# Splitting two small matmul passes in a DMA-fed start-up, and giving the last Q blocks four PSUM banks

## The chip, the cores and the metric

The kernel runs on one core of a Trainium2 chip. The metric is the device time of that core in microseconds (us). Most runs of one kernel agree within 0.3%.

## The reference, cut to what matters

One transformer block on 2048 tokens of width 1024, in bf16: linear attention with 32 heads, then a gated MLP, both with a layernorm whose scale and shift come from a condition vector.

```python
mod = (silu(c) @ w_mod)                         # six rows of 1024: sa, ca, ga, sb, cb, gb
h = layernorm(x) * (1 + ca) + sa
q, k, v = split(h @ wqkv)
pq, pk = phi(q), phi(k)                         # phi(t) = where(t > 0, t + 1, exp(t)) + 1e-6
kv = einsum('bhsd,bhse->bhde', pk, v); z = pk.sum(s)
o = (pq @ kv) / (pq @ z + 1e-6)
x = x + ga * (o @ wo)
h = layernorm(x) * (1 + cb) + sb
x = x + gb * ((gelu(h @ w_gate) * (h @ w_up)) @ w_down)
```

## The kernel before

Every instruction is put in its engine's stream in program order; a wait is added wherever an instruction touches bytes that another engine or a transfer wrote or still reads. So the order of the lines below is the order on TensorE.

**Start-up.** Nothing can be multiplied before weights and x have come from memory. The scale and shift of the first layernorm are needed as columns (one value per partition), in four quarters of 256 features. Quarter `q` has two weight tiles, 512 KB each: shift (`t` = 0, issued first) and scale (`t` = 1). A column pass is 32 matmuls with one column each (shortened here, as all code of this document):

```python
def mod_cols(q, bank, ts=(1, 0)):               # scale first, then shift
    for t in ts:
        for b in range(2):
            col = MC0 + q * 4 + t * 2 + b
            for dc in range(NDC):               # 8
                matmul(PS(bank, col, col + 1), WMQ[q][:, dc, t, b*P:(b+1)*P], SILUT[:, dc:dc+1], ...)
```

`mod_copy(q)` (VectorE) takes the four columns out of PSUM, and `mod1` (VectorE) scales and shifts the transposed h1T. Only then may the K matmuls of this quarter's two 128-feature slices (`dc` = 2q, 2q+1) run. The transfers are issued in this order: ..., wmq2 (shift, scale), wk 4, wk 5, wmq3 (shift, scale), wk 6, wk 7, wv (first half of its columns in two pieces, then the second half, 1 MB), x of chunks 4 to 7, wq. The end of the start-up, where `k_tiles` and `k_part` are K matmuls of some slices and `kb0` says which bank each K tile of chunks 0 to 3 is collected in:

```python
k_part(0, [3]); k31([2, 3])
mod_cols(2, 4)
mod_copy(2, 4)
k_tiles([3], [(2, 0), (2, 1)])
k_tiles([2, 3], [(3, 0)])
mod1(0, 1, 4, 5); mod1(1, 3, 4, 5); mod1(0, 4, 5, 6)
k_tiles([4, 5], [(0, 0), (0, 1), (1, 0), (1, 1)])
k_tiles([4], [(2, 0), (2, 1)])
mod_cols(3, 4)
mod_copy(3, 4)
mod1(0, 1, 6, 8); mod1(1, 3, 6, 8)
k_tiles([5], [(2, 0), (2, 1)])
k_tiles([4, 5], [(3, 0)])
for (c_, jg), b in kb0.items(): kv_mm(c_, "k", jg, b, [6, 7])     # 14 matmuls
k31([4, 5, 6, 7]); k31(list(range(NDC)), MC0, 512)                # k31: chunk 3, second half of K
# ... evictions of K ...
for c_ in range(4):                              # V tiles: (chunk, half of the columns)
    for vc, jg in (((0, 0), (1, 0)), ((0, 1), (1, 1)), ((2, 0), (2, 1)), ((3, 0), (3, 1)))[c_]:
        b = nb(); kv_mm(vc, "v", jg, b, range(NDC)); v_evac(vc, jg, b)
    # ... kvacc(c_ - 1) if c_ >= 1
```

**The last Q blocks.** PSUM has eight banks; banks 5 to 7 hold the accumulated KV until VectorE has copied it out (kvbd). It is then transposed by a DMA (kvt), and W2 = KV x wo is made, two banks a pair. `den` is the denominator pq @ z for two of the four groups of 512 tokens (a "pair" of groups); VectorE takes its reciprocal, which comes back broadcast by DMA (`rb_load`) for `pq_scale`. `wo_chunk` multiplies 128 tokens of pq with W2. Twelve Q blocks are still to do, ten of them after `kvt`; a Q block is 8 matmuls into one bank, followed by ScalarE's exponential and two VectorE instructions (the last of them is `pq`):

```python
def q_next(evac=True):
    sg, qc = q_todo.pop(0)
    b = (0, 1, 2, 3)[qn[0]] if qn[0] < 4 else qn[0] % 2     # from the fifth on: banks 0 and 1
    qn[0] += 1
    q_block(sg, qc, evac, b)

first_q = q_next(False); kvacc(NCH - 1); zcols(); q_evac(*first_q)
q_next()
den(0, 3); kvbd(); kvt(); rb_load(0); rb_load(1)
q_next(); q_next()
for u in range(NG):                              # 8
    q_next()
    if u >= 2: w2_pair(u - 2 + (u == 7))         # banks 2 and 3
    if u == 6: w2_pair(5, 4)                     # banks 4 and 5
    # ... pq_scale on VectorE
w2_pair(NG - 1, 4)
# ...
for c_ in range(12):
    wo_chunk(c_, 6 if c_ == 0 else 2 * (c_ % 2)) # two banks a chunk
    if c_ == 0: den(1, 4); rb_load(2)
```

Of the kernel before, what the change touches and what calls it, by code (L numbers as in the profile page):

```python
# [18 lines left out]
NG = 8  # L19
# [195 lines left out]
def bass_adaLN_cond__linear_attn_block__geglu_ffn__prompt_kernel(  # L215
# [15 lines left out]
    with ExitStack() as es:  # L231
# [85 lines left out]
        def r_sm(name):  # L317
            return [(SMO[name], SMO[name] + SMSZ[name], name)]
# [13 lines left out]
        def r_h1(sg, k0=0, k1=NDC, s0=0, s1=SGW):  # L332
            return r_t8(H1O[sg], f"h1T{sg}", k0, k1, s0, s1)
# [7 lines left out]
        def r_w(off, name, dc, c0=0, c1=D):  # L341
            return [(off + (dc * D + c0) * 2, off + (dc * D + c1) * 2, name)]
# [14 lines left out]
        def r_wmq(i, t):  # L357
            return [(MSO[i] + (dc * 2 + t) * 512, MSO[i] + (dc * 2 + t + 1) * 512, f"wmq{i}") for dc in range(NDC)]
# [33 lines left out]
        def pr(b):  # L392
            return [(b * 2048, (b + 1) * 2048)]

        def PS(b, c0=0, c1=512):
            return ps_all[:, b * 512 + c0: b * 512 + c1]
# [187 lines left out]
        def mod1(c0, n, dc0=0, dc1=NDC):  # L584
            sg, ci = divmod(c0, CPG)
            mods(H1, r_h1, sg, sc1, ci * P, (ci + n) * P, dc0, dc1, "h1")
# [8 lines left out]
        def mod_cols(q, bank, ts=(1, 0)):  # L595
            o = None
            rng = [(bank * 2048 + (MC0 + q * 4) * 4, bank * 2048 + (MC0 + q * 4 + 4) * 4)]
# [3 lines that stand above are left out]
                    for dc in range(NDC):  # L601
                        o = sch.op(T, lambda e, t=t, b=b, dc=dc, col=col: e.matmul(
                            PS(bank, col, col + 1), WMQ[q][:, dc, t, b * P:(b + 1) * P], SILUT[:, dc:dc + 1],
                            start=(q == b == dc == 0 and t == 1), stop=(dc == NDC - 1), skip_group_check=True),
                            rd=r_wmq(q, t) + r_sm("siluT"), pwr=(rng if dc == 0 else ()), note=f"mod{q}.{t}.{b}.{dc}")
            for t_ in rng:
                sch.ps.set_writer(t_[0], t_[1], o)

        def mod_copy(q, bank):
            rng = [(bank * 2048 + (MC0 + q * 4) * 4, bank * 2048 + (MC0 + q * 4 + 4) * 4)]  # L610
            sch.op(V, lambda e: e.tensor_tensor(MODT[:, q * 4:q * 4 + 4], PS(bank, MC0 + q * 4, MC0 + q * 4 + 4), ADD4[:, :], ALU.add),
                   prd=rng, rd=r_sm("add4"), wr=r_smc("modt", q, 16), note=f"modcp{q}")
# [65 lines left out]
        def kv_mm(c_, kind, jg, bank, dcs):  # L678
            sg, ci = divmod(c_, CPG)
            W_, off, name = (WK, OFF_WK, "wk") if kind == "k" else (WV, OFF_WV, "wv")  # L680
            o = None
            for dc in dcs:
                o = sch.op(T, lambda e, dc=dc: e.matmul(PS(bank), H1[sg][:, dc, ci * P:(ci + 1) * P], W_[:, dc, jg * 512:(jg + 1) * 512],  # L683
                                                        start=(dc == 0), stop=(dc == NDC - 1)),
                           rd=r_h1(sg, dc, dc + 1, ci * P, (ci + 1) * P) + r_w(off, name, dc, jg * 512, (jg + 1) * 512),
                           pwr=(pr(bank) if dc == 0 else ()), note=f"{kind} c{c_} jg{jg} dc{dc}")
            if dcs[-1] == NDC - 1:
                pset_writer(bank, o)
# [26 lines left out]
        def nb():  # L715
            b = bank_i[0] % bank_i[1]
            bank_i[0] += 1
            return b
# [37 lines left out]
        def k31(dcs, c0=0, c1=MC0):  # L756
            rng = [(4 * 2048 + c0 * 4, 4 * 2048 + c1 * 4)]
            for dc in dcs:
                o = sch.op(T, lambda e, dc=dc: e.matmul(PS(4, c0, c1), H1[0][:, dc, 3 * P:4 * P], WK[:, dc, 512 + c0:512 + c1],
                                                        start=(c0 > 0 and dc == 0), stop=(dc == NDC - 1), skip_group_check=True),  # L760
                           rd=r_h1(0, dc, dc + 1, 3 * P, 4 * P) + r_w(OFF_WK, "wk", dc, 512 + c0, 512 + c1),
                           pwr=(rng if dc == 0 else ()), note=f"k c3 jg1 dc{dc} {c0}")
            if dcs[-1] == NDC - 1:
                sch.ps.set_writer(*rng[0], o)

        def k_tiles(dcs, tiles):
            for dc in dcs:
                for c_, jg in tiles:
                    kv_mm(c_, "k", jg, kb0[c_, jg], [dc])
# [47 lines left out]
        mod1(3, 1, 0, 4)  # L817
        k_part(0, [3])
        k31([2, 3])
        mod_cols(2, 4)  # L820
        mod_copy(2, 4)
        k_tiles([3], [(2, 0), (2, 1)])
        k_tiles([2, 3], [(3, 0)])
        mod1(0, 1, 4, 5)
        mod1(1, 3, 4, 5)
        mod1(0, 4, 5, 6)
        k_tiles([4, 5], [(0, 0), (0, 1), (1, 0), (1, 1)])
        k_tiles([4], [(2, 0), (2, 1)])
        mod_cols(3, 4)
        mod_copy(3, 4)  # L830
        mod1(0, 1, 6, 8)
        mod1(1, 3, 6, 8)
        k_tiles([5], [(2, 0), (2, 1)])
        k_tiles([4, 5], [(3, 0)])
        for (c_, jg), b in kb0.items():
            kv_mm(c_, "k", jg, b, [6, 7])
        k31([4, 5, 6, 7])
        k31(list(range(NDC)), MC0, 512)
        for (c_, jg), b in kb0.items():
            k_evac(c_, jg, b)  # L840
# [1 line left out]
        for c_ in range(4):  # L842
            for vc, jg in (((0, 0), (1, 0)), ((0, 1), (1, 1)), ((2, 0), (2, 1)), ((3, 0), (3, 1)))[c_]:
                b = nb()
# [58 lines left out]
        for c_ in range(4, NCH):  # L903
# [23 lines left out]
            for jg in range(2):  # L927
                b = nb()
# [3 lines left out]
            for jg in range(2):  # L932
                b = nb()
# [37 lines left out]
        def w2_pair(g, b0=2):  # L971
            for half in range(2):
                b = b0 + half
                sch.op(T, lambda e, b=b, half=half: e.matmul(PS(b), KVT[:, g, :], WO[:, g, half * 512:(half + 1) * 512], start=True, stop=True),  # L974
                       rd=R_KVT + [(OFF_WS + g * 2048 + half * 1024, OFF_WS + g * 2048 + (half + 1) * 1024, "wo")], pwr=pr(b), note=f"w2 {g}.{half}")
            sch.op(A, lambda e: e.activation(W2[:, g, :], ps_all[:, b0 * 512:(b0 + 2) * 512], ACTF.Copy),
                   prd=pr(b0) + pr(b0 + 1), wr=r_w(OFF_WK, "w2", g), note=f"w2cp{g}")
# [44 lines left out]
        qn = [0]  # L1022

        def q_next(evac=True):
            sg, qc = q_todo.pop(0)
            b = (0, 1, 2, 3)[qn[0]] if qn[0] < 4 else qn[0] % 2
            qn[0] += 1
            q_block(sg, qc, evac, b)
            return sg, qc, b
# [13 lines left out]
        for u in range(NG):  # L1043
            q_next()
            if u >= 2:
                w2_pair(u - 2 + (u == 7))
            if u == 6:
                w2_pair(5, 4)
            if u in (3, 4):
                pq_scale(0, 0, GH[u - 3])  # L1050
            if u in (6, 7):
                pq_scale(0, 1, GH[u - 6])
        w2_pair(NG - 1, 4)
        assert not q_todo

        wd_q = [0]
# [11 lines left out]
        def wo_chunk(c_, b0):  # L1068
            sg, ci = divmod(c_, CPG)
            last = [None, None]  # L1070
            for g in range(NG):
                for half in range(2):
                    last[half] = sch.op(T, lambda e, g=g, half=half: e.matmul(  # L1073
                        PS(b0 + half), PQ[sg][:, g, ci * P:(ci + 1) * P], W2[:, g, half * 512:(half + 1) * 512],
                        start=(g == 0), stop=(g == NG - 1)),
                        rd=r_pq(sg, g, g + 1, ci * P, (ci + 1) * P) + r_w(OFF_WK, "w2", g, half * 512, (half + 1) * 512),
                        pwr=(pr(b0 + half) if g == 0 else ()), note=f"wo c{c_} g{g} h{half}")
            for half in range(2):
                pset_writer(b0 + half, last[half])
            sch.op(V, lambda e: e.tensor_tensor(XALL[:, c_, :], ps_all[:, b0 * 512:(b0 + 2) * 512], XALL[:, c_, :], ALU.add),  # L1080
                   prd=pr(b0) + pr(b0 + 1), rd=r_x(c_), wr=r_x(c_), note=f"x1 c{c_}")
# [16 lines left out]
        stream_pair(0, 0)  # L1098
        stream_pair(0, 1)
        for c_ in range(12):  # L1100
            wo_chunk(c_, 6 if c_ == 0 else 2 * (c_ % 2))
            if c_ == 0:
                den(1, 4)
                rb_load(2)
            if 1 <= c_ <= 8:
                pq_scale(1 + (c_ - 1) // 4, (c_ - 1) // 2 % 2, GH[(c_ - 1) % 2])
            if c_ == 4:
                rb_load(3)
                sch.op(V, lambda e: e.tensor_scalar(CB1T[:, :], CBT[:, :], 1.0, None, op0=ALU.add), rd=r_sm("cbT"), wr=r_sm("cb1T"))
            if c_ in (10, 11):  # L1110
                pq_scale(3, 0, GH[c_ - 10])
            if c_ < 4:
                ln2_a(c_, False)
            if c_ == 9:
                mod2(0, 2)
                mod2(2, 2)
# [201 lines left out]
```

## Time and profile before

837.68 us median of 6 runs (837.29 to 839.5). The page of the profiled run (a run of its own, 838.21 us):

```profile
span 836.0 us, 11356 instructions
## 1 busy us (share of the span) xinstructions
PE 828.2 (99%) x4189; PEld 383.2 (46%) x4189; DVE 512.4 (61%) x898; ACT 334.7 (40%) x554; POOL 36.7 (4%) x91
```

TensorE (PE) is busy nearly all the time. A matmul of 512 columns is listed at 379 ns, but it overlaps its neighbours: what counts is the distance from start to start. In the timeline below, the 32 V matmuls listed from 30.97 us take 7.07 us, and the next instruction starts 6.90 us after the first, 0.216 us each. This is what the Trainium skill, "TensorE: Matmul & The Clock Gate", section "Back-to-back issue gap", gives (N/2.4 + 2.5 ns, so 215.8 ns for N = 512). The kernel can therefore gain only where this pace is broken.

The timeline of TensorE, end of the start-up (start in us, length in us, engine, line, operation, output <- inputs, shape, how many; in brackets the idle time before the first and what ended it). L602 is the column pass, L683 K or V, L759 is `k31`:

```profile
19.87 0.79 PE L759 MATMUL ps_all<-wk,h1T 128*128 128x496 bf16 x3
21.05 0.95 PE L602 MATMUL ps_all<-siluT,wmq 128*128 128x1 bf16 x32 [0.38 <-DMA wmq<-in_w_mod_dram]
21.86 3.18 PE L683 MATMUL ps_all<-wk,h1T 128*128 128x512 bf16 x14
25.23 0.95 PE L602 MATMUL ps_all<-siluT,wmq 128*128 128x1 bf16 x32 [0.19 <-DMA wmq<-in_w_mod_dram]
26.05 4.04 PE L683 MATMUL ps_all<-wk,h1T 128*128 128x512 bf16 x18
29.93 1.19 PE L759 MATMUL ps_all<-wk,h1T 128*128 128x496 bf16 x12
30.97 7.07 PE L683 MATMUL ps_all<-wv,h1T 128*128 128x512 bf16 x32
```

There are two holes. The three `k31` matmuls from 19.87 are paced out at 20.50, but the pass of quarter 2 starts at 21.05. The 14 K matmuls from 21.86 are paced out at 24.88, but the pass of quarter 3 starts at 25.23. Both are ended by a DMA of `wmq`. The bracket is smaller than the hole of start times (0.55 and 0.35 us) because a modelled end of a matmul hangs over.

The third hole, TensorE again, then VectorE in the same stretch:

```profile
174.85 7.08 PE L724 MATMUL ps_all<-h1T,wq 128*128 128x512 bf16 x32
182.45 1.89 PE L724 MATMUL ps_all<-h1T,wq 128*128 128x512 bf16 x8 [0.52 <-DVE pq L675]
```

```profile
181.16 0.42 DVE L673 TENSOR_SCALAR eb<-eb 128x512 f32<-128x512 f32 x1
181.61 0.69 DVE L675 SCALAR_TENSOR_TENSOR pq<-ps_all,eb 128x512 bf16<-128x512 f32 x1
```

The 32 matmuls (four Q blocks) from 174.85 are paced out at 181.76. The next block starts at 182.45, when VectorE has taken the block in the same bank out of PSUM (`pq`, 181.61 + 0.69). That is 0.69 us. The waits of TensorE that belong to these holes (total us, times, longest):

```profile
PE ps_all L602 <- DMA wmq<-in_w_mod_dram: 1.8, 3, 1.2
...
PE ps_all L724 <- DVE pq L675: 0.5, 1, 0.5
```

The first line also has a wait of 1.24 us at 10.15 us, for quarter 0, which the change does not touch.

### The profile page before, as it was taken

The page shows a single profiled execution, that of the slowest core. Times are in us where ns is not written, and L with a number is a line of the kernel's source. Part 1 is how long each engine was busy: PE and PEld are TensorE (multiplying, and loading weights), DVE is VectorE, ACT ScalarE, POOL GpSimd, SP SyncE. Part 2 cuts the span into 40 slices and gives each one's busy share as a digit, 9 for nine tenths or more (in the row PEclk, how much of TensorE's full clock was granted, in tenths as well). Part 3 has the DMA queues.
Part 4 walks back from the last instruction along what each step waited for, and adds up shares of the span by engine and source line. Part 5 has one row for each costly group of instructions (what it writes and reads, how often), then busy time and mean ns, then how long its engine had stood idle before and what let it go on. Part 6 is the DMA issues. An engine that isn't in the chain of part 4 may idle for free.

```text
span 836.0 us, 11356 instructions
## 1 busy us (share of the span) xinstructions
PE 828.2 (99%) x4189; PEld 383.2 (46%) x4189; DVE 512.4 (61%) x898; ACT 334.7 (40%) x554; POOL 36.7 (4%) x91
## 2 busy tenths in 40 slices
PE   7999999999999999999999999999999999999998
PEld 3444444444444444444444444444444444444445
DVE  6678877687785577753566665355556535555512
ACT  2357777436423355420444442045554104455300
POOL 2011111000200000000000000000000000000000
PEclk9999999999999999999999999999999999999999
DMA  9984422239696779180555533055553305555000
GB/s 281 331 245 112 91 76 80 74 88 237 145 240 197 226 208 273 30 189 26 158 151 151 152 101 75 20 158 152 152 151 102 76 20 161 155 153 143 7 19 26
DMA packets 185182, 113.48 MB, mean 136 GB/s; under 512 B 36636, under 2 KB 176164, under 8 KB 184104
## 3 DMA queue, kind: packets, MB, share of 16 engines
q1 hardware_dynamic: 185112, 112.76, 50.1%
q8 instruction: 33, 0.54, 0.3%
q14 instruction: 21, 0.17, 0.1%
q10 hardware_dynamic: 16, 0.00, 0.0%
HBM read 100.67 MB, written 4.47 MB: 126 GB/s over the span
## 4 chain that ended last, share of the span: by engine, by line
PE 96%; SPq 2%; DMA 1%; DVE 0%; issue 0%
PE ps_all L1158 23%; PE ps_all L1130 23%; PE ps_all L1133 23%; PE ps_all L683 12%; PE ps_all L1073 7%; PE ps_all L724 6%; SPq L448 1%; PE ps_all L705 1%; SPq L453 1%; DMA wmq<-in_w_mod_dram 1%; PE ps_all L974 0%; PE ps_all L986 0%; SPq L442 0%; DVE kvbd L964 0%; DVE eb L673 0%
## 5 line engine op out<-in xcount | busy, mean ns | idle before, releaser
L1130 PE MATMUL ps_all<-h2T,wg 128*128 128x512 bf16 x896 | 339.6, 379 | 0.0
L1133 PE MATMUL ps_all<-h2T,wu 128*128 128x512 bf16 x896 | 339.6, 379 | 0.0
L1158 PE MATMUL ps_all<-wd,yT 128*128 128x512 bf16 (+3 forms) x952 | 194.2, 366 | 0.0
L1141 ACT ACTIVATE q<-ps_all 128x512 f32<-128x512 f32 x112 | 66.9, 597 | 225.7 <-PE ps_all L1130 224.4
L1158 PEld LDWEIGHTS ps_all<-wd,yT 128*128 128x128 bf16 x952 | 90.1, 98 | 103.7 <-issue 0.2
L1130 PEld LDWEIGHTS ps_all<-h2T,wg 128*128 128x128 bf16 x896 | 87.7, 98 | 105.8 <-issue 0.2
L1133 PEld LDWEIGHTS ps_all<-h2T,wu 128*128 128x128 bf16 x896 | 87.7, 98 | 105.7
L1146 DVE SCALAR_TENSOR_TENSOR ww<-th,guh 128x512 f32<-128x512 f32 x112 | 77.5, 692 | 77.9 <-ACT th L1145 77.9
L1143 DVE SCALAR_TENSOR_TENSOR ww<-q,ps_all 128x512 f32<-128x512 f32 x112 | 76.9, 687 | 77.5 <-ACT guh L1142 77.4
L1145 ACT ACTIVATE th<-ww 128x512 f32<-128x512 f32 x112 | 70.5, 629 | 87.0 <-DVE ww L1143 87.0
L1163 DVE TENSOR_TENSOR ps_all<-ps_all,gbb 128x512 f32<-128x512 f32 (+3 forms) x34 | 22.7, 667 | 94.6 <-PE ps_all L1158 94.6
L1148 DVE TENSOR_TENSOR yT<-ww,ps_all 128x512 bf16<-128x512 f32 x112 | 76.9, 686 | 3.8
L1142 ACT ACTIVATE guh<-ps_all 128x512 f32<-128x512 f32 x112 | 66.3, 592 | 0.0
L724 PE MATMUL ps_all<-h1T,wq 128*128 128x512 bf16 x256 | 58.5, 379 | 0.5 <-DVE pq L675 0.5
L683 PE MATMUL ps_all<-wv,h1T 128*128 128x512 bf16 x256 | 57.7, 379 | 0.0
L672 ACT ACTIVATE eb<-ps_all 128x512 f32<-128x512 f32 x64 | 37.5, 599 | 50.4 <-PE ps_all L724 24.1
L683 PE MATMUL ps_all<-wk,h1T 128*128 128x512 bf16 x248 | 56.6, 379 | 0.3 <-DVE h1T L565 0.2
L1073 PE MATMUL ps_all<-w,pq 128*128 128x512 bf16 x256 | 56.2, 379 | 0.0
L673 DVE TENSOR_SCALAR eb<-eb 128x512 f32<-128x512 f32 x64 | 27.1, 423 | 25.9 <-ACT eb L672 25.6
L1073 PEld LDWEIGHTS ps_all<-w,pq 128*128 128x128 bf16 x256 | 25.0, 98 | 30.2 <-issue 0.2
L683 PEld LDWEIGHTS ps_all<-wv,h1T 128*128 128x128 bf16 x256 | 24.9, 98 | 29.5
L724 PEld LDWEIGHTS ps_all<-h1T,wq 128*128 128x128 bf16 x256 | 24.3, 98 | 27.9 <-issue 1.2
(93 smaller groups left out, 474.4 us busy)
## 6 DMA issues: line engine op xcount, KB each, us to landing
wg<-in_B_w_gate_dram SPq DMA_DIRECT2D x56, 512.0 KB, 4.0
wu<-in_B_w_up_dram SPq DMA_DIRECT2D x56, 512.0 KB, 5.3
rb<-scr_rd SPq DMA_DIRECT2D x32, 256.0 KB, 7.2
wd<-in_B_w_down_dram SPq DMA_DIRECT2D x7, 1024.0 KB, 8.3
wmst<-in_w_mod_dram SPq DMA_DIRECT2D x6, 1024.0 KB, 6.7
wmq<-in_w_mod_dram SPq DMA_DIRECT2D x8, 512.0 KB, 7.4
out_dram<-xall SPq DMA_DIRECT2D x31, 128.0 KB, 1.7
xall<-in_A_x_dram SPq DMA_DIRECT2D x3, 1024.0 KB, 11.0
```

The source lines that it names most:

```text
L683: o = sch.op(T, lambda e, dc=dc: e.matmul(PS(bank), H1[sg][:, dc, ci * P:(ci + 1) * P], W_[:, dc, jg * 512:(jg + 1) * 512], start=(dc == 0 ...
L724: o = sch.op(T, lambda e, dc=dc: e.matmul(PS(b), WQ[:, dc, qc * P:(qc + 1) * P], H1[sg][:, dc, :], start=(dc == 0), stop=(dc == NDC - 1)), ...
L1073: last[half] = sch.op(T, lambda e, g=g, half=half: e.matmul(PS(b0 + half), PQ[sg][:, g, ci * P:(ci + 1) * P], W2[:, g, half * 512:(half + ...
L1130: og = sch.op(T, lambda e, dc=dc: e.matmul(PS(bg), WG[slot][:, dc, e_ * P:(e_ + 1) * P], H2[sg][:, dc, :], start=(dc == 0), stop=(dc == ND ...
L1133: ou = sch.op(T, lambda e, dc=dc: e.matmul(PS(bu), WU[slot][:, dc, e_ * P:(e_ + 1) * P], H2[sg][:, dc, :], start=(dc == 0), stop=(dc == ND ...
L1141: sch.op(A, lambda e: e.activation(Q1[j][:, :], PS(bg), ACTF.Square, scale=math.sqrt(GELU_A)), prd=pr(bg), wr=rq, note=f"q1 {fc}")
L1142: ogh = sch.op(A, lambda e: e.activation(GUH[j][:, :], PS(bg), ACTF.Copy, scale=0.5), prd=pr(bg), wr=rg, note=f"gh {fc}")
L1143: sch.op(V, lambda e: e.scalar_tensor_tensor(WW[j][:, :], Q1[j][:, :], 1.0, PS(bg), op0=ALU.add, op1=ALU.mult), rd=rq, prd=pr(bg), wr=rw, ...
L1145: sch.op(A, lambda e: e.activation(TH[j][:, :], WW[j][:, :], ACTF.Tanh, scale=GELU_C), rd=rw, wr=rt, note=f"th {fc}")
L1146: sch.op(V, lambda e: e.scalar_tensor_tensor(WW[j][:, :], TH[j][:, :], 1.0, GUH[j][:, :], op0=ALU.add, op1=ALU.mult), rd=rt + rg, wr=rw, n ...
L1148: sch.op(V, lambda e: e.tensor_tensor(YT[:, fc, :], WW[j][:, :], PS(bu), ALU.mult), rd=rw, prd=pr(bu), wr=r_yt(fc), note=f"yT {fc}")
L1158: o = sch.op(T, lambda e, b=b, fc=fc, c0=c0, c1=c1, n=n: e.matmul(PS(b, 0, n), YT[:, fc, ci * P:(ci + 1) * P], WDT[fc // 4][:, fc % 4, c0:c1],
```

## The change

Its intent: cover the waits for the column weights by splitting the pass at the landing of its two tiles and putting K matmuls between the halves, and let no Q block wait for a bank. For the latter, Q takes banks 0 to 3 in turn, and the W2 pairs take banks 4 and 5 or 6 and 7, alternating where two pairs follow each other. No matmul is added or taken away. The diff, with unchanged lines cut:

```diff
-        mod_cols(2, 4)
+        mod_cols(2, 4, (0,))
+        k_tiles([3], [(2, 0)])
+        mod_cols(2, 4, (1,))
         mod_copy(2, 4)
-        k_tiles([3], [(2, 0), (2, 1)])
+        k_tiles([3], [(2, 1)])
         k_tiles([2, 3], [(3, 0)])
         ...
         k_tiles([4, 5], [(0, 0), (0, 1), (1, 0), (1, 1)])
+        mod_cols(3, 4, (0,))
         k_tiles([4], [(2, 0), (2, 1)])
-        mod_cols(3, 4)
+        k31([4, 5])
+        k_tiles([5], [(2, 0)])
+        mod_cols(3, 4, (1,))
         mod_copy(3, 4)
         ...
-        k_tiles([5], [(2, 0), (2, 1)])
+        k_tiles([5], [(2, 1)])
         ...
-        k31([4, 5, 6, 7])
+        k31([6, 7])
@@ the last Q blocks
-            b = (0, 1, 2, 3)[qn[0]] if qn[0] < 4 else qn[0] % 2
+            b = qn[0] % 4
...
-                w2_pair(u - 2 + (u == 7))
+                w2_pair(u - 2 + (u == 7), 6 if u in (3, 5) else 4)
             if u == 6:
-                w2_pair(5, 4)
+                w2_pair(5, 6)
...
-        w2_pair(NG - 1, 4)
+        w2_pair(NG - 1, 6)
...
-            wo_chunk(c_, 6 if c_ == 0 else 2 * (c_ % 2))
+            wo_chunk(c_, 2 * (c_ % 2))
```

## The prediction

> **What bounds the kernel.** TensorE. The page's first part has PE busy 828.2 of 836.0 us, clock 1.0. A 128x512 matmul is listed at 379 ns, but in the timeline starts follow each other every 0.216 us, which agrees with the Trainium skill's "TensorE: Matmul & The Clock Gate", section "Back-to-back issue gap" (N/2.4 + 2.5 ns, 215.8 ns at N = 512). From 26 us to the end TensorE runs at that pace, with one real hole. Only holes can be won, and the change aims at three:
>
> 1. 21.05 us: the 32 one-column matmuls of quarter 2 start 0.55 us late, released by the DMA of their weights (second half landed 21.00, first half 18.91).
> 2. 25.23 us: the same for quarter 3, 0.35 us (second half landed 25.18).
> 3. 182.45 us: a Q block of the last group starts 0.69 us late, released by VectorE's pq: it needs bank 0; VectorE is behind by its 1.75 us reciprocal and 1.28 us of kvbd.
>
> No matmul is added or removed; 16 one-column matmuls take 0.41 us.
>
> **Start-up, by the landing times of before.** The first half of quarter 2 can start at 20.50, one K matmul follows, the second half starts at 21.13 (landed) and ends at 21.54, not 21.86. Fewer K matmuls now cover the copy and first scaling on VectorE, so a wait below 0.1 us may appear. Eight K matmuls end near 24.0. The first half of quarter 3 is not waited for in the trace; I estimate its landing at 23.4 from the packets. Then 1.48 us of work brings TensorE to about 25.5, just after the second half's landing. V starts at about 30.2 instead of 30.97. Gain: 0.8 us, at worst 0.5.
>
> **The tail of Q.** With four banks in turn, that block takes bank 2, drained at 180.2, and it starts at once. W2 pairs move to banks 4 to 7, which kvbd has released by 179.1. The next limit is the transposed KV, landed 182.54; w2's first matmul would come at about 183.5 (with the start-up gain both shift). Gain: 0.69 us.
>
> **Does it last?** Everything after is paced by TensorE or moves with it. VectorE's chain of nine K evictions starts only about 0.35 us earlier, but V, the KV accumulation and the next K tile have over 1 us of slack. Around 187 us VectorE will wait some 0.5 us for the broadcast reciprocals (rb); four banks cover that. The h2T transposes, paced by DMA, land at 231.5, before the scaling at 233.2; FFN has slack in its weight loads.
>
> **Prediction.** Gain about 1.4 us (0.17%): 836.2 us, range 835.5 to 837.0. Faster by over 2%: 0.5%; within 2%: 99%; slower by over 2%: 0.5%.
>
> **What would show it.** Waits list: PE's wait for wmq falls from 1.8 us towards 1.2 (only the first quarter's); PE's wait for pq (0.5) disappears. Timeline: V starts at 30.1 to 30.4; no hole of TensorE between 174.9 and 196 minus the shift; den of the second pair starts about 1.5 us earlier; FFN's first matmul near 237.4 instead of 238.79; the span near 834.6.
>
> **What would make it wrong.** The first half of quarter 3 lands after 24.0 us; transfers land at other times in this run ; wk's last tiles, landed at about 26, stop dc 6 and 7; the KV transpose becomes the new wait at w2, taking back part of 0.69; rb's later landing stops the first wo chunks; a different chip.

## The result, and the profile after

836.48 us median of 6 runs (835.96 to 837.4), against 837.68 (837.29 to 839.5): 1.2 us less. The ratio is 0.9984, 95% interval 0.9971 to 0.9997. Ratios here are the mean time of one kernel's fast runs over that of the other's of the same rounds, so not quite the ratio of the medians. The page, where the trace has 4109 of the 4189 matmuls (each missing record looks like a gap of 0.216 us, so holes are taken from the weight loads, which are all there; this run is one of the six, 837.12 us):

```profile
span 835.0 us, 11277 instructions
## 1 busy us (share of the span) xinstructions
PE 824.6 (99%) x4109; PEld 384.2 (46%) x4189; DVE 512.6 (61%) x898; ACT 334.5 (40%) x554; POOL 35.6 (4%) x91
```

TensorE in the start-up of the changed kernel, to be held against the lines from 19.87 to 30.97 of before:

```profile
19.93 0.54 PE L602 MATMUL ps_all<-siluT,wmq 128*128 128x1 bf16 x16
20.33 0.38 PE L683 MATMUL ps_all<-wk,h1T 128*128 128x512 bf16 x1
21.13 0.55 PE L602 MATMUL ps_all<-siluT,wmq 128*128 128x1 bf16 x16 [0.42 <-DMA wmq<-in_w_mod_dram]
21.55 2.65 PE L683 MATMUL ps_all<-wk,h1T 128*128 128x512 bf16 x10
24.03 0.54 PE L602 MATMUL ps_all<-siluT,wmq 128*128 128x1 bf16 x16
...
25.50 0.54 PE L602 MATMUL ps_all<-siluT,wmq 128*128 128x1 bf16 x16
25.90 0.81 PE L683 MATMUL ps_all<-wk,h1T 128*128 128x512 bf16 x3
26.87 2.98 PE L683 MATMUL ps_all<-wk,h1T 128*128 128x512 bf16 x13 [0.17 <-DVE h1T L565]
...
30.31 7.32 PE L683 MATMUL ps_all<-wv,h1T 128*128 128x512 bf16 x31
```

Five things are to be seen. The first half of quarter 2 (19.93) does not wait. The second (21.13) still does: one K matmul is not enough to reach its landing at 21.09. Neither half of quarter 3 waits (24.03 and 25.50). At 26.87 there is a new small wait for VectorE's scaling. It is about 0.1 us in the weight loads, since one of the matmuls just before is missing. A like wait of 0.1 us, for the scaling of quarter 2, is inside the row from 21.55: its 11 matmuls (10 recorded) last until 24.03, and 11 steps of 0.216 us would end at 23.93. And V starts at 30.31 instead of 30.97, but its 32 matmuls (31 recorded) then take 7.32 us instead of 7.07: the 17th, the first that needs the second half of wv's columns, starts 0.26 us late, at 34.02, and that half landed at 33.93.

The last Q blocks, and the wait of TensorE for `wmq`:

```profile
174.45 8.81 PE L724 MATMUL ps_all<-h1T,wq 128*128 128x512 bf16 x39
183.09 0.59 PE L979 MATMUL ps_all<-wo,kvt 128*128 128x512 bf16 x2
```

```profile
PE ps_all L602 <- DMA wmq<-in_w_mod_dram: 0.4, 1, 0.4
```

The five Q blocks before the first W2 pair now run in one piece (40 matmuls, 39 recorded, 174.45 to 183.09, which is 8.64 us or 0.216 each). The wait for `pq` is gone from the list. On VectorE the broadcast reciprocals (`rb`) brought a new wait, which TensorE does not feel:

```profile
188.91 1.29 DVE L1023 TENSOR_TENSOR pq<-pq,rb 128x512 bf16<-128x512 bf16 x2 [1.61 <-DMA rb<-scr_rd]
```

Four landmarks sum it up. The den of the first pair (weight loads) moved from 173.86 to 173.46, the den of the second from 199.81 to 198.72, the first FFN weight load from 238.66 to 237.58, and the span from 836.0 to 835.0. So the bank part gave its 0.68 us, but of the 0.65 us that V was early only 0.40 were left at the first den.

### The profile page after: what moved, and what is told of

It is laid out like the page before. It is cut to its first block, busy times and chain, and to the rows that moved or that the text cites. A ratio compares the mean times of both kernels' runs of the same rounds, so it can differ in the third digit from the quotient of the medians.

```text
span 835.0 us, 11277 instructions
## 1 busy us (share of the span) xinstructions
PE 824.6 (99%) x4109; PEld 384.2 (46%) x4189; DVE 512.6 (61%) x898; ACT 334.5 (40%) x554; POOL 35.6 (4%) x91
## 4 chain that ended last, share of the span: by engine, by line
PE 95%; SPq 1%; DMA 1%; issue 1%; DVE 1%; ACT 1%; ACTq 0%
PE ps_all L1138 23%; PE ps_all L1163 23%; PE ps_all L1135 22%; PE ps_all L683 12%; PE ps_all L1078 7%; PE ps_all L724 7%; DMA wmq<-in_w_mod_dram 1%; PE ps_all L705 1%; SPq L448 1%; PE ps_all L979 0%; SPq L453 0%; DVE ww L1151 0%; DVE ww L1148 0%; PE ps_all L991 0%; ACT th L1150 0%
## 5 line engine op out<-in xcount | busy, mean ns | idle before, releaser
L1135 PE MATMUL ps_all<-h2T,wg 128*128 128x512 bf16 x859 | 325.6, 379 | 0.0
L1078 PEld LDWEIGHTS ps_all<-w,pq 128*128 128x128 bf16 x256 | 25.0, 98 | 30.2 <-issue 0.2
```

Source lines behind the costliest of these rows:

```text
L1078: last[half] = sch.op(T, lambda e, g=g, half=half: e.matmul(PS(b0 + half), PQ[sg][:, g, ci * P:(ci + 1) * P], W2[:, g, half * 512:(half + ...
L1135: og = sch.op(T, lambda e, dc=dc: e.matmul(PS(bg), WG[slot][:, dc, e_ * P:(e_ + 1) * P], H2[sg][:, dc, :], start=(dc == 0), stop=(dc == ND ...
```

## The experiments

Theory A: the two parts are independent gains and each is whole at the end; what is missing in the profile was lost to the landing times of transfers in that single run (D). Rivals: one of the parts gives everything (B), a new wait behind the banks takes part back (C), or the change itself delays the transfers (E).

Every profile was read with the same marks. L is the landing of quarter 2's second tile (the time at which the transfer's completion reached its semaphore). "V" is V's first weight load. "wv" is the landing of wv's second half. "V wait" is the time from V's to the following Q's first weight load, less the 15.14 us that it has without a hole. "den to den" goes from the first pair's first weight load to the second's. The other stretches are the same in all 14 profiles: 127.78 us from that Q to the first den, 38.85 from the second den to FFN, 597.38 from there to the end, each within 0.01. Quarter 3's second tile landed 4.13 to 4.19 us after L in all 14, so with the old start-up, whose last wait is for that tile, V - L is fixed as well.

| run | start-up | Q and W2 banks | L | V - L | wv - L | V wait | den to den | span | span - L |
|---|---|---|---|---|---|---|---|---|---|
| before | old | old | 21.00 | 9.95 | 11.66 | 0 | 25.95 | 836.04 | 815.04 |
| e7_w2_moved | old | W2 moved only | 21.11 | 9.94 | 12.51 | 0 | 25.95 | 836.14 | 815.03 |
| e5_q2_split | quarter 2 split | old | 20.71 | 9.93 | 12.82 | 0 | 25.96 | 835.74 | 815.03 |
| e6_q3_split | quarter 3 split | old | 20.30 | 9.70 | 12.58 | 0 | 25.95 | 835.10 | 814.80 |
| e2_banks | old | new | 21.01 | 9.93 | 13.22 | 0 | 25.27 | 835.35 | 814.34 |
| e1_startup | new | old | 21.08 | 9.19 | 12.50 | 0 | 25.95 | 835.37 | 814.28 |
| after | new | new | 21.09 | 9.20 | 12.84 | 0.26 | 25.27 | 834.95 | 813.87 |
| e3_after_again | new | new | 21.38 | 9.20 | 12.28 | 0 | 25.27 | 834.99 | 813.61 |
| e11_after_third | new | new | 20.83 | 9.19 | 12.27 | 0 | 25.27 | 834.44 | 813.61 |
| e4_v_order | new, V reordered | new | 21.39 | 9.20 | 13.29 | 0 | 25.27 | 835.00 | 813.62 |
| e12_v_order_again | new, V reordered | new | 21.42 | 9.20 | 13.10 | 0 | 25.27 | 835.03 | 813.61 |
| e8_w2_one_pair | new | Q new, W2 in one pair | 21.57 | 9.20 | 13.44 | 0.85 | 28.08 | 838.84 | 817.27 |
| e9_late_wv | new, wv late | new | 21.01 | 9.20 | 15.29 | 4.20 | 25.27 | 838.82 | 817.81 |
| e10_late_wv_v_order | new, wv late, V reordered | new | 20.98 | 9.20 | 15.41 | 1.10 | 25.27 | 835.70 | 814.72 |

### Each part alone, and the whole once more

`e1_startup` has only the start-up hunks of the diff, `e2_banks` only the others, and `e3_after_again` is the changed kernel unaltered.

> Start-up part alone (both column passes split), banks as before. Theory A (two independent gains; the start-up gives 0.4 to 0.7 us, the banks 0.69): V's first matmul near 30.3 us, the first KV accumulation 0.4 to 0.8 us before the 37.87 us of before, and the hole of 0.69 us before the seventh Q block of the last group is still there, so the time falls by 0.4 to 0.8 us only. Rival B (the start-up gain is eaten later, the whole gain comes from the banks): the first KV accumulation is early, but the den of the second pair starts within 0.1 us of before's 199.81, and the time falls by under 0.2 us.

> Bank part alone, start-up as before. Theory A: den of the first pair at before's distance, the hole of 0.69 us gone, den of the second pair 0.7 us earlier relative to den of the first pair (25.27 us after it instead of 25.95), time down by 0.6 to 0.75 us. Rival C (the KV transpose or the reciprocal broadcasts become the new wait and take part of it back): a new hole of TensorE at w2 or at the first wo chunk, and den to den above 25.4 us.

> The changed kernel once more, for a second profile. The first one has a wait of 0.26 us at the 17th V matmul, because the second half of wv landed at 33.93 us instead of 32.66. Theory D (the landing moves from run to run by itself, before's 32.66 and 33.93 are both ordinary): the landing lies anywhere between 32.5 and 34 in the eight profiles of this study, and V's wait is there only where it is over about 33.7. Rival E (the change delays it): about 33.9 in each kernel with the split passes and about 32.7 in each without. Time 1.0 to 1.4 us below before.

The hole stands in the run with the start-up part alone (TensorE, then the same stretch with the banks alone):

```profile
174.18 7.08 PE L724 MATMUL ps_all<-h1T,wq 128*128 128x512 bf16 x31
181.79 1.89 PE L724 MATMUL ps_all<-h1T,wq 128*128 128x512 bf16 x8 [0.52 <-DVE pq L675]
```

```profile
174.84 8.81 PE L724 MATMUL ps_all<-h1T,wq 128*128 128x512 bf16 x39
```

Kernels are compared only within the same rounds. Times, with the kernel before at 838.03 us (837.39 to 840.17, 9 runs): start-up alone 837.51 (837.02 to 837.91), ratio 0.999, interval 0.9976 to 1.0003. Banks alone 837.51 (836.63 to 839.23), 0.9992, 0.9979 to 1.0006. Both 837.17 (836.57 to 837.65), 0.9985, 0.9972 to 0.9997. The times say that each part gives something like half, but not how much. The table does. The start-up alone takes span - L from 815.04 to 814.28 (0.76), the banks alone to 814.34 (0.70), both to 813.61 (1.43), so they add up. Rival B falls, since the start-up's gain is still whole at the end of the run. Rival C falls as well: den to den is 25.27 with no new hole.

The wait at V's 17th matmul did not return in the second run of the changed kernel (`e3_after_again`), where wv's second half landed 12.28 us after L instead of 12.84. (The landings spread wider than the 32.5 to 34 us expected, up to 34.67 us in `e4`, and 34.23 us was harmless in `e2`, whose V is late: what decides is the distance from L, not the time.) The line of V in this run has the old length:

```profile
30.60 7.07 PE L683 MATMUL ps_all<-wv,h1T 128*128 128x512 bf16 x31
```

The changed kernel ran once more with the last experiments, `e11_after_third`:

> The changed kernel a third time. V 9.20 us after the landing of quarter 2's second half, den to den 25.27 us. A wait at the 17th V matmul if and only if wv's second half lands over about 12.65 us after quarter 2's second half (in the ten profiles so far: 11.7 to 13.4 us); the span is then before's minus 0.74, minus 0.69, plus that wait, plus the difference of quarter 2's landing.

wv landed 12.27 us after L, there was no wait, and span - L is 813.61 again. The time is 836.71 us (836.45 to 837.47) against 838.17 (837.67 to 838.5), ratio 0.9986, interval 0.9969 to 1.0003.

### Another order of V

The first V tile that needs wv's second half is moved one tile back, and the tile of chunk 2 that needs the first half takes its place:

```diff
-  (((0, 0), (1, 0)), ((0, 1), (1, 1)), ((2, 0), (2, 1)), ((3, 0), (3, 1)))[c_]
+  (((0, 0), (1, 0)), ((2, 0), (0, 1), (1, 1)), ((2, 1),), ((3, 0), (3, 1)))[c_]
```

> The changed kernel with the V tiles in another order, so that the second half of wv is first needed one tile (1.73 us) later. If V's wait for that half is what took back part of the start-up gain: no hole of TensorE among the V matmuls, first KV accumulation no later than in the changed kernel plus the extra 1.73 us of a V tile that is moved ahead of it, the Q matmuls after V up to 0.26 us earlier than in the changed kernel relative to V's first matmul, and time 0 to 0.3 us lower than the changed kernel. If the wait is a symptom of something else: a hole of about the same size elsewhere.

> The changed kernel with the other V order a second time: no hole among the V matmuls wherever wv lands (up to about 14.4 us after quarter 2's second half), so span equals 813.7 us plus that landing, within 0.1. Time not distinguishable from the changed kernel's by these rounds, since 0 to 0.9 us is at stake in single runs.

In its two profiles wv landed 13.29 and 13.10 us after L, later than in the profile of the changed kernel that had to wait, and there is no hole; the 40 V matmuls run in one piece to the first KV accumulation:

```profile
30.64 8.79 PE L683 MATMUL ps_all<-wv,h1T 128*128 128x512 bf16 x40
```

The span less L is 813.62 and 813.61, as expected. The times are 837.16 us (836.43 to 837.5; changed kernel 837.17) and 837.02 (836.28 to 837.45; changed kernel 836.71, before 838.17), so no difference can be shown in the time. What is shown is that the order takes the wait away in the trace.

### wv late on purpose

To see the wait at a size that cannot be chance, the 1 MB of wv is issued behind the 1 MB of x that follows it. `e10` has the other V order too.

```diff
-        w_dma(WV, OFF_WV, "wv", 2, 512, 1024)
         x_dma(4, 8)
+        w_dma(WV, OFF_WV, "wv", 2, 512, 1024)
```

> The changed kernel with the second half of wv issued behind the 1 MB of x that follows it, so that it lands about 2.7 us later on purpose (that is what the x transfer takes in the profiles), about 15.3 us after quarter 2's second half. If V waits for that half alone, the 17th V matmul, due 12.7 us after that landing, gets a hole of about 2.6 us, and nothing later makes it up: span and time 2.3 to 2.7 us above the changed kernel. If there is slack behind V: less.

> The same late wv with the other V order: first use one tile later, so the hole is about 1.73 us smaller, 0.8 to 1.1 us; time 1.6 to 1.8 us below the run with the late wv and the old order.

TensorE in V, old order and then new order:

```profile
30.23 3.61 PE L683 MATMUL ps_all<-wv,h1T 128*128 128x512 bf16 x16
36.40 4.88 PE L683 MATMUL ps_all<-wv,h1T 128*128 128x512 bf16 x15 [2.55 <-DVE eb L673]
```

```profile
30.20 5.34 PE L683 MATMUL ps_all<-wv,h1T 128*128 128x512 bf16 x24
36.49 3.61 PE L683 MATMUL ps_all<-wv,h1T 128*128 128x512 bf16 x16 [0.94 <-DVE pk L675]
```

The profile names VectorE as the releaser in both, but wv landed at 36.31 and 36.40, just before the starts at 36.40 and 36.49. The instruction waits for several semaphores, and the name is not reliable here. That V stands on wv is shown by moving wv alone. With the other order the hole is 1.10 us instead of 2.72. The times are 839.86 us (838.71 to 840.98) and 837.94 us (837.88 to 838.08), against 836.71 for the changed kernel: 3.15 us more with the old order where 2.3 to 2.7 was expected, and 1.92 less with the other order where 1.6 to 1.8 was expected. The four runs of the old order are of two kinds, though (see below), and their median lies between them.

The old order was expected to lose about 2.6 us in V and lost 4.20. The stretches of the late-wv run (busy time and count by engine, then the granted TensorE clock, DMA share and GB/s) tell why:

```profile
core 0: us, PE busy (x) PEld busy (x) DVE busy (x) ACT busy (x) POOL busy (x), PEclk, DMA share, GB/s
33.00:36.00 3.00, 0.84 (x4) 0.20 (x2) 2.90 (x7) 0.60 (x1) 0.00 (x0) 1.00 1.10 350
36.00:37.00 1.00, 0.60 (x2) 0.29 (x3) 1.00 (x2) 0.00 (x0) 0.00 (x0) 0.52 1.10 346
37.00:38.00 1.00, 1.00 (x3) 0.30 (x2) 0.91 (x3) 0.00 (x0) 0.00 (x0) 0.50 1.10 348
38.00:39.00 1.00, 1.00 (x4) 0.39 (x3) 0.32 (x2) 0.00 (x0) 0.55 (x1) 0.50 1.11 350
39.00:40.00 1.00, 1.00 (x5) 0.41 (x4) 0.98 (x2) 0.19 (x1) 0.00 (x0) 0.78 1.01 318
40.00:41.00 1.00, 1.00 (x6) 0.49 (x5) 0.91 (x3) 0.41 (x1) 0.00 (x0) 1.00 0.48 139
```

After a hole of 2.72 us (from 33.68, where the sixteenth V matmul is paced out, to 36.40) TensorE ran at half clock until 39.44; the record of the clock has this half-speed interval from 36.03 to 39.44, 3.41 us long. The first eight matmuls after the hole took 3.21 us from start to start (36.40 to 39.61) in place of 1.73, which makes the other 1.48 us. It does not come each time: of the four runs two (one of them the traced run) took 840.98 us at a mean clock of 0.998, and two 838.71 and 838.74 at 1.0. The latter have no trace, and 2.25 us is more than the 1.48 that the half clock cost in the trace, so their landings, and perhaps their holes, differed too. In the traces, the holes of 1.10 us (`e10`), 0.85 and 1.4 us (`e8`) left the clock at 1.0.

### One split at a time

```diff
 e5: only the hunk of quarter 2      e6: only the hunks of quarter 3 (with k31 in two parts)
```

> Only the pass of quarter 2 is split. In six profiles V's first matmul starts at a fixed distance from the landing of quarter 2's second half: 9.94 us in the kernels with the old start-up, 9.20 in those with the new one. Theory A2 (the next wait, for quarter 3's weights, swallows it): the hole before quarter 3's pass grows from 0.35 to about 0.8 us and V still starts 9.9 us after that landing, so no gain. Rival B2 (the splits are worth something each on their own): about 9.4 to 9.6 us.

> Only the pass of quarter 3 is split (with the early k31). Theory A2: the hole before quarter 3's second half is gone, since TensorE comes there about 0.4 us after the landing; V starts about 9.6 us after the landing of quarter 2's second half, a gain of 0.3 to 0.35 us of the 0.74 of both. Rival B2 (quarter 3's split is the whole gain): 9.2 us.

With quarter 2 split alone, TensorE is early and then waits longer for quarter 3. With quarter 3 split alone, quarter 2's wait is still there and quarter 3's is gone (the first run's lines, then the second's):

```profile
21.17 3.08 PE L683 MATMUL ps_all<-wk,h1T 128*128 128x512 bf16 x13
24.92 0.95 PE L602 MATMUL ps_all<-siluT,wmq 128*128 128x1 bf16 x32 [0.67 <-DMA wmq<-in_w_mod_dram]
```

```profile
20.34 0.95 PE L602 MATMUL ps_all<-siluT,wmq 128*128 128x1 bf16 x32 [0.25 <-DMA wmq<-in_w_mod_dram]
...
25.21 0.54 PE L602 MATMUL ps_all<-siluT,wmq 128*128 128x1 bf16 x16
```

In the first, the 13 K matmuls from 21.17 are paced out near 24.1, and the pass comes at 24.92, right after the landing at 24.87: a hole of about 0.8 us where before had 0.35. V - L is 9.93, as in the kernel before. So in this profile the split of quarter 2 is worth nothing by itself. Quarter 3 alone gives 0.24 us (9.94 to 9.70; 0.3 to 0.35 were expected), both give 0.74. The times, 837.77 and 837.52 against 838.08, ratios 0.9993 and 0.9992 with intervals on both sides of 1, cannot tell this.

### What the banks need

`e7` moves W2 away from banks 2 and 3 for the third to seventh Q block of the loop over `u`, but leaves Q on two banks. `e8` is the changed kernel with all W2 pairs in banks 4 and 5.

```diff
 e7, against the kernel before
-                w2_pair(u - 2 + (u == 7))
+                w2_pair(u - 2 + (u == 7), 2 if u == 7 else 6 if u in (3, 5) else 4)
-                w2_pair(5, 4)
+                w2_pair(5, 6)
 e8, against the changed kernel
-                w2_pair(u - 2 + (u == 7), 6 if u in (3, 5) else 4)
+                w2_pair(u - 2 + (u == 7), 4)
-                w2_pair(5, 6)
+                w2_pair(5, 4)
-        w2_pair(NG - 1, 6)
+        w2_pair(NG - 1, 4)
```

> Kernel before, with the W2 pairs of the third to seventh Q block in banks 4 to 7, but the Q blocks still on two banks. If the hole is Q's wait for its own bank: it stays at about 0.69 us, den of the second pair 25.95 us after den of the first, time as before. If W2's place in banks 2 and 3 were the reason: the hole shrinks and the distance falls to 25.3 us. Also a seventh start-up profile of the old kind: V 9.94 us after the landing of quarter 2's second half, wherever that falls between 21.0 and 21.5 us.

> The changed kernel, with all W2 pairs in banks 4 and 5. The Q blocks never wait, but where two W2 pairs follow each other (seventh and eighth Q block) the second waits for the copy of the first: copies take 0.97 us and start behind a 0.60 us exponential, so two new holes of about 1.2 us each, den of the second pair 27.4 to 27.9 us after den of the first instead of 25.27, time 1.0 to 1.4 us above the kernel before. If the alternation is not needed: 25.3 us and the time of the changed kernel.

The hole of `e7` is where it was. In `e8` the second of two successive pairs waits for ScalarE's copy of the first:

```profile
182.56 1.89 PE L724 MATMUL ps_all<-h1T,wq 128*128 128x512 bf16 x8 [0.53 <-DVE pq L675]
```

```profile
192.80 0.59 PE L979 MATMUL ps_all<-wo,kvt 128*128 128x512 bf16 x2
194.63 0.60 PE L979 MATMUL ps_all<-wo,kvt 128*128 128x512 bf16 x2 [1.23 <-ACT w L981]
```

`e7`: den to den 25.95, time 838.34 us (837.78 to 841.57) against 838.08. `e8`: den to den 28.08, so the two waits cost 2.81 us together, 1.4 each where 1.2 had been estimated; time 840.14 us (839.81 to 841.0), 2.06 above before where 1.0 to 1.4 had been expected. In its profile span - L is 2.23 us above before's, and 0.85 of that is V's wait for wv; the other 1.38 are as expected. `e7` is a weak test by itself, since in program order the hole comes before the first W2 pair; with `e2`, where the hole went with four banks for Q, it shows what is needed. So Q's bank is what the hole was about, and the alternation of the W2 pairs is what makes the freed banks usable.

## Why the prediction was right or wrong

- **Total.** 836.2 us predicted (835.5 to 837.0), 836.48 measured. That the time itself came within 0.3 us is partly luck, as the median of the kernel before alone was 837.68, 838.03, 838.08 and 838.17 us. The gain of 1.4 us is 1.43 at equal landings (815.04 to 813.61), and 1.2, 0.86 and 1.46 us by the medians.
- **The banks, 0.69 us.** Right in mechanism and size: den to den fell from 25.95 to 25.27, also with the part alone. The KV transpose did not become the next wait.
- **The start-up, 0.8 us.** Right: V - L fell from 9.94 to 9.20, 0.74 us. The remaining 0.06 us is within the prediction's own rounding (30.97 to 30.2 is 0.77). The small waits for VectorE's scaling came twice, about 0.1 us each (quarters 2 and 3), where the prediction named one, for quarter 2. The route was not quite as told. TensorE was 0.57 us earlier than in the kernel before when it reached quarter 2 in this run, and so still waited about 0.6 us for the second half.
- **"Everything after is paced by TensorE or moves with it": the step that failed, though the total still came out.** The slack of "over 1 us" that the prediction gives V is that behind VectorE's K evictions, and it was there: in the profile after, V's first bank was free at 29.08 us, 1.23 before V used it. But the landing of wv's second half is not paced by TensorE and does not move with it, and the prediction did not look at it. V had 1.76 us of slack for wv's second half in the trace of before (needed at 34.42, landed at 32.66). The start-up's gain takes 0.74 of it, and the rest is not fixed: wv - L runs from 11.7 to 13.4 us over the 12 profiles where its issue was not moved, and the new start-up needs it by about 12.65. In the profile after it cost 0.26 us, in `e8` 0.85, in the other three with the old V order nothing. The prediction listed "transfers land at other times in this run" as a risk, in general; it did not say which transfer had become the next limit.
- **The single marks.** V at 30.1 to 30.4: 30.31. No hole among the Q blocks: none. den of the second pair "about 1.5 us earlier": 1.09. FFN's first matmul "near 237.4": its weight load moved by 1.08 instead of 1.4. Span "near 834.6": 835.0. The last three fall short for the same reasons. The two terms promised 1.49 and the den moved by 1.09: 0.26 went to wv, 0.09 to an L that was later than before's, and 0.06 is the size of the start-up term, to the rounding. PE's wait for wmq "towards 1.2": 0.4, since this time the wait at quarter 0, which the change does not touch, did not come. VectorE's wait for rb "some 0.5 us": 1.61, and, as said, without effect on TensorE. And the pace of 0.216 us agrees with the formula that the prediction names, but the section gives that for an isolated gap and not for a stream.

What stays open. L lies at 21.00 to 21.11 in three profiles with the old start-up and at 20.83 to 21.57 in nine with the new one, 20.71 and 20.30 with one split: nothing shows that the change moves it (rival E; wv's landing speaks against it as well, with 34.23 us under the old start-up in `e2` and 33.10 under the new one in `e11`), but so few profiles cannot exclude a tenth or two. And four of 32 runs with the old start-up whose clock was recorded took 839.2 to 841.6 us at a mean clock of 0.998, like the two slow runs with the late wv, while none of 33 with the new start-up (late wv left out) did. One half-clock interval like that in the late-wv trace fits the clock of 0.998, but by my estimate from its 3.41 us it costs at most 1.7 us, and these runs are 1.7 to 3.2 us above the median of their kernel. The holes of the old start-up may be what brings it on. Those runs have no trace, so this is only argued, and not the whole of it. They are also among the runs on which the ratios of the experiments rest, which is one more reason to read the gains from the traces.

## What to carry to other kernels

A split or reorder that fills the wait for one transfer is worth only what the next transfer leaves. Cover successive waits together, then ask which landing is next and move its first use back if that is free, as the V order did here. When a start-up is fed by DMA, one profile's landings are a sample: measure the distance from the landing to the work that it releases, which here repeated within 0.02 us while the landings moved by more than 1 us. For PSUM, count the banks of all that is in flight together; giving one stream more banks needs the other stream moved, and alternated.

## What the Trainium skill lacked or had wrong

- "TensorE: Matmul & The Clock Gate", section "What's actually happening" (Part 1): it has the clock fall to half after at least one idle window of about 3.4 us. In the trace of `e9`, the half-speed interval was 3.41 us long, the length of the page's window, but it began only 2.35 us into a hole of 2.72 us, so there was no idle stretch of 3.4 us before it. Another run of the four took the same time at the same mean clock; the holes of the other two are not known. Holes of 0.85 to 1.4 us in traces did not do it.
- The same page, section "Back-to-back issue gap": it says that sustained pairs of weight load and matmul reach about 131 ns each at N = 512, and that N/2.4 + 2.5 overstates it. In this kernel such pairs follow each other every 216 ns (40 of them in 8.64 us), the value of the formula. In the trace of before the median of 3690 distances between 512-column matmuls is 216 ns, and none between such pairs is below 215.
- "DMA: Bandwidth & Descriptors", section "Latency and other measured facts": it has latencies (HBM access 0.2 us on average, 2 us at high load), but no spread of the landing of one and the same transfer from run to run, and no other page that I found has it. Here, 14 profiles have the second tile of quarter 2 landing between 20.30 and 21.57 us, and wv's second half between 32.66 and 35.01 us where its issue was not moved.
